# Attention and a gated MLP on one core: exponentials turned in 32x32 blocks on VectorE, v products in plain fp32 on eight array tiles

## The chip, the core and the metric

The kernel runs on one core of one Trainium2 chip. The core has five engines with a queue each: TensorE (PE in the profile; its weight loads are the row PEld), VectorE (DVE), ScalarE (ACT), GpSimd (POOL) and SyncE (SP), which here only issues DMAs. SBUF and PSUM have 128 partitions; TensorE reads SBUF and writes PSUM. The metric is the device time of one execution in microseconds (us).

## What is computed

Eight batches, eight heads, 576 positions, head size 64. Attention runs for each head, and its output feeds an MLP for each batch in which the positions are mixed by a 576x576 matrix.

```python
q_rot, k_rot = (rotate(q), rotate(k))
scores = scale * np.matmul(q_rot, k_rot.transpose(0, 1, 3, 2))
scores = scores - np.max(scores, axis=-1, keepdims=True)
attn = np.exp(scores)
attn = attn / (np.sum(attn, axis=-1, keepdims=True) + 1e-09)
x = np.matmul(attn, v)
...
h = np.maximum(x @ w_in, 0.0)
u, v = (h[..., :d_ff // 2], h[..., d_ff // 2:])
v_n = (v - mu) / np.sqrt(var + 1e-06)
v_s = np.einsum('ts,bsd->btd', w_spatial, v_n) + b_spatial[None, :, None]
out = (u * v_s) @ w_out
```

## The kernel before

**Tiling.** Two heads make a pair, so there are 32 pairs, four to a batch. A pair's scores are nine tiles of 128 query rows by 576 keys: four for each head, and a ninth that holds the last 64 queries of both. A score tile is a PSUM buffer of the pool `sc` (two of them). TensorE fills it (L542; for pair 0 L552), VectorE takes the negated row maximum `nmx` (L563), and ScalarE writes the exponentials `e` to SBUF and sums them (L565).

**Values.** The product with v contracts over keys, so keys must lie on partitions, while `e` has queries there. TensorE therefore turns `e` in 128x128 blocks by matmuls with an identity (`tp`, L582) into PSUM. To keep full precision in fp32r products, ScalarE rounds the turned block to `eh` (L593), and VectorE writes the rest to `el` (L312, a line shared by all such remainders). v is split in the same way into `vs` (ScalarE, then GpSimd L443). `pv` (L606) then sums `eh` by both parts of v, and `el` by the high part. The 576 queries of both heads are worked in three chunks of 384 columns. At the end of a chunk ScalarE copies one half of `pv` (L623) and VectorE adds the other (L621). The first four pairs (`PLAIN = 4`) skip the split: their products (L679) are plain fp32, 64 output rows wide, from turned blocks that ScalarE or VectorE copies out of PSUM (L648, L650). Then GpSimd multiplies by the inverse sums (L716), and `x` is split for the MLP.

**MLP.** For each batch there are four stages of fp32r products: `pa` (L750), `pb` (L773), `pc` (L791) and `pd` (L806), in PSUM banks of the pool `pm`. The turned blocks `tp` use the same pool.

**Order.** No queue is filled at run time by readiness. The program lists operations with a cost, a key (due time) and the buffers that they take. `Program.run` plays this list through once while the program is built: whenever an engine is free, it takes the ready operation with the lowest key whose buffers can be placed. The order so found is fixed for each engine, and each engine works through it in order. Pair i has keys from 20*i on, and the MLP of batch b from 80*b + 90.

```python
SLOTS = {
    "stage": 2, "lk": 1, "vraw": 2, "vs": 2, "e2": 4, "e1": 2, "eh": 7, "rb": 1, "x32": 1, "xg": 7, "m": 4,
    "small": 3, "nmx": 3, "rt": 2, "sc": 2, "pv": 1, "pm": 3,
}
```

The costs in that list are the author's figures for the planner. They are not measurements, and no time in this document is taken from them.

Of the kernel before, what the change touches and what calls it, by code (L numbers as in the profile page):

```python
# [9 lines left out]
F32 = mybir.dt.float32  # L10
# [6 lines left out]
P = 128  # L17
# [20 lines left out]
PSUM = {"sc": 1024, "pv": 512, "pm": 512}  # L38
# [6 lines left out]
CHUNKS = [  # L45
# [22 lines left out]
K_LOAD, K_ROPE, K_SUM, K_HIQ, K_LOQ, K_LOK, K_STACK, K_STACK2, K_V, K_VLO = 27, 8, 8, 9, 9, 11, 30, 8, -2, -9
# [31 lines left out]
class Op:  # L100
    def __init__(self, costs, key, f, new, port):
        self.costs, self.key, self.f, self.new, self.port = costs, key, f, new, port
        self.eng, self.late = None, 0
        self.waits, self.after, self.bufs = 0, [], []


class Program:
# [30 lines left out]
    def run(self, make):  # L138
# [22 lines left out]

        busy = dict.fromkeys(LATENCY, False)
# [5 lines left out]
        while events:  # L168
# [23 lines left out]
            for e in LATENCY:  # L192
# [3 lines left out]
                while ready[e] and not chosen:  # L196
# [27 lines left out]
def tile_attention_gated_mlp(  # L224
# [48 lines left out]
    ident = T([P, P], F32, "ident")  # L273
# [10 lines left out]
    ks = [T([P, TW + S], F32R, f"ks{a}") for a in range(2)]  # L284
# [95 lines left out]

    def prepare(i):
# [4 lines left out]
        st = [Buf("stage", [P, 2 * S + TW], F32, f"st{i}_{j}") for j in range(2)]  # L386
        lk = Buf("lk", [P, TW + S], F32R, f"lk{i}")
        vr = Buf("vraw", [P, NQ, 2, D], F32, f"vr{i}")
        vs = Buf("vs", [P, NQ, 2, 2, D], F32R, f"vs{i}")
        prepped.append((lk, vr if i < PLAIN else vs))  # L390

        def hi(j, rows=slice(0, P)):

            return st[j][rows, S:2 * S + TW * j].bitcast(F32R)
# [16 lines left out]
        op(DMA, 910, key - K_LOAD + 1, lambda: load(vr.tile, v[b, hp]), w=[vr], new=[vr])  # L411
# [28 lines left out]
        if i < PLAIN:  # L440
            return
# [507 lines left out]
```

## Time and profile before

The median of 3 runs is 967.17 us (965.44 to 967.69). The profiled execution's span is 963.6 us, 3.6 us below that median.

| engine | busy us | share of the span | main work |
|---|---|---|---|
| PE | 934.0 | 97% | MLP products, scores, turning `e`, v products |
| ACT | 738.2 | 77% | exponentials, rounding `eh` |
| DVE | 656.6 | 68% | row maxima, remainders `el` |
| POOL | 601.1 | 62% | rotation, remainders of q, k, x |

The table is to be read with care. A share is a mean over three parts: about 100 us with the first four pairs and no MLP, some 800 us with attention and MLP side by side, and a last part with the MLP of the last batch alone. PE's busy time also counts a matmul's pipeline, so overlapping matmuls each show more than their share; how far apart they start says more.

### The profile page before, as it was taken

How to read it: one execution, taken by the hardware profiler on the slowest of the kernel's cores; microseconds unless marked ns; L12 is line 12 of the kernel's file. 1: busy time of each engine (PE TensorE's matmuls, PEld its weight loads, DVE VectorE, ACT ScalarE, POOL GpSimd, SP SyncE). 2: the span in 40 equal slices, each digit the busy share in tenths (PEclk: the TensorE clock that was granted, in tenths of full speed). 3: DMA queues.
4: the chain of work that ended last, by engine and by line, in shares of the span. 5: the costliest groups of instructions: out<-in, count | busy, mean ns of one | idle time of the engine just before them, and what ended most of it. 6: DMA issues, size and time to landing. Idle time of an engine off the chain costs nothing.

```text
span 963.6 us, 19472 instructions
## 1 busy us (share of the span) xinstructions
PE 934.0 (97%) x6614; PEld 856.2 (89%) x6614; DVE 656.6 (68%) x1461; ACT 738.2 (77%) x1835; POOL 601.1 (62%) x526
## 2 busy tenths in 40 slices
PE   4988899999999999999999999999999999999998
PEld 2555589999899989999899998999889998999998
DVE  5898686766867677665776658676676766866331
ACT  4887788777987779777897779877798678976452
POOL 6775766576758557774765766666586765672121
PEclk9998999999999999999999999999999999999999
DMA  7775634455354554346444444445524455430101
GB/s 273 240 233 170 191 106 124 130 125 140 103 136 127 159 141 114 102 116 171 124 135 118 117 149 122 127 122 152 149 74 132 123 167 144 110 83 13 62 1 50
DMA packets 56037, 124.64 MB, mean 129 GB/s; under 512 B 13185, under 2 KB 13441, under 8 KB 55938
## 3 DMA queue, kind: packets, MB, share of 16 engines
q1 hardware_dynamic: 55938, 123.40, 46.0%
q8 instruction: 53, 0.87, 0.4%
q14 instruction: 46, 0.38, 0.1%
HBM read 66.03 MB, written 9.58 MB: 78 GB/s over the span
## 4 chain that ended last, share of the span: by engine, by line
PE 75%; ACT 13%; DVE 6%; issue 2%; DMA 2%; POOL 1%; SPq 0%; ACTq 0%; DVEq 0%; POOLq 0%
PE sc L542 13%; PE pc L791 12%; PE pv L606 11%; PE tp L582 11%; PE pd L806 10%; PE pb L773 9%; PE pa L750 5%; ACT e L565 4%; ACT eh L593 2%; DVE nmx L563 2%; ACT vv L837 2%; PE pv L679 1%; PE sc L552 1%; DVE el L312 1%; ACT st L309 1%
## 5 line engine op out<-in xcount | busy, mean ns | idle before, releaser
L593 ACT ACTIVATE eh<-tp 128x384 fp32r<-128x384 f32 (+1 forms) x504 | 217.9, 434 | 85.4 <-PE tp L582 68.2
L312 DVE TENSOR_TENSOR el<-tp,eh 128x384 fp32r<-128x384 f32 x336 | 185.9, 554 | 101.9 <-ACT eh L593 88.0
L563 DVE TENSOR_REDUCE nmx<-sc 128x1 f32<-128x576 f32 x288 | 214.9, 749 | 47.9 <-PE sc L542 40.7
L565 ACT ACTIVATE e<-sc,nmx 128x576 f32<-128x576 f32 x288 | 213.2, 741 | 40.1 <-DVE nmx L563 36.0
L582 PE MATMUL tp<-ident,e 128*128 128x128 f32 (+1 forms) x1176 | 195.6, 273 | 1.3 <-DVE eh L312 0.4
L401 POOL TENSOR_TENSOR st<-st,tabq 128x576 f32<-128x576 f32 x62 | 87.9, 1435 | 134.0 <-DMA st<-in_qk_dram 104.5
L582 PEld LDWEIGHTS tp<-ident,e 128*128 128x128 f32 (+1 forms) x1176 | 145.8, 138 | 16.3 <-issue 3.0
L606 PE MATMUL pv<-eh,vs 128*128 128x384 f32 (+1 forms) x560 | 154.5, 317 | 1.5 <-ACT x L685 1.4
L791 PE MATMUL pc<-wsp,vn 128*128 128x288 f32 x768 | 143.1, 303 | 0.0
L773 PE MATMUL pb<-x,wi 128*128 128x288 f32 x768 | 141.8, 306 | 0.6 <-ACT u L776 0.5
L806 PE MATMUL pd<-g,wo 128*128 128x288 f32 x768 | 141.3, 303 | 0.0
L542 PE MATMUL sc<-ks,qs 128*128 128x288 f32 x620 | 133.1, 304 | 4.8 <-ACT e L565 4.3
L750 PE MATMUL pa<-wi,x 128*128 128x512 f32 x448 | 133.2, 407 | 0.0
L542 PE MATMUL sc<-lk,qz 128*128 128x288 f32 x558 | 120.4, 297 | 0.0
L806 PEld LDWEIGHTS pd<-g,wo 128*128 128x128 f32 x768 | 114.0, 189 | 3.4 <-DVE el L312 0.4
L791 PEld LDWEIGHTS pc<-wsp,vn 128*128 128x128 f32 x768 | 114.6, 189 | 1.8
L773 PEld LDWEIGHTS pb<-x,wi 128*128 128x128 f32 x768 | 112.1, 189 | 4.4 <-PE pb L773 1.1
L542 PEld LDWEIGHTS sc<-ks,qs 128*128 128x128 f32 x620 | 100.8, 190 | 15.9 <-ACT e L565 7.2
L606 PE MATMUL pv<-el,vs 128*64 128x384 f32 (+1 forms) x448 | 113.9, 295 | 0.1
L606 PEld LDWEIGHTS pv<-eh,vs 128*128 128x128 f32 x560 | 97.7, 188 | 7.8 <-DVE x L621 2.0
L716 POOL TENSOR_TENSOR x<-x,rb 128x576 f32<-128x576 f32 x32 | 45.9, 1435 | 79.2 <-DVE x L621 73.1
L312 DVE TENSOR_TENSOR eh<-tp,eh 64x256 fp32r<-64x256 f32 (+1 forms) x168 | 59.8, 356 | 51.8 <-ACT eh L593 28.2
(166 smaller groups left out, 1540.6 us busy)
## 6 DMA issues: line engine op xcount, KB each, us to landing
st<-in_qk_dram SPq DMA_DIRECT2D x64, 576.0 KB
ks<-st SPq DMA_DIRECT2D x124, 160.0 KB
qs<-st SPq DMA_DIRECT2D x124, 144.0 KB
vr<-in_v_dram SPq DMA_DIRECT2D x32, 320.0 KB
qz<-st SPq DMA_DIRECT2D x62, 144.0 KB
out_dram<-ob SPq DMA_DIRECT2D x31, 288.0 KB
ws<-in_w_spT_dram SPq DMA_DIRECT2D x2, 576.0 KB
tabs<-in_tab_dram SPq DMA_DIRECT2D x1, 576.0 KB
```

Source lines behind the costliest of these rows:

```text
L312: eng.tensor_tensor(out=lo, in0=src, in1=hi.bitcast(F32), op=ALU.subtract)
L401: f = lambda e: e.tensor_tensor(out=st[j][:, cols], in0=st[j][:, cols], in1=(tabs if j else tabq)[:, cols], op=ALU.mult)
L542: nc.tensor.matmul(pt[:, c * 512:c * 512 + HALF], lhsT=lhsT, rhs=rhs[:, k0 + c * HALF:k0 + (c + 1) * HALF], start=(n == 0), stop=(n == len ...
L563: op(DVE, 665, key + K_MAX, lambda: nc.vector.tensor_reduce(out=nmx.tile, in_=tops(), op=ALU.max, axis=AX.XY, negate=True), r=[pt], w=[nmx ...
L565: op(ACT, 730, key + K_EXP, lambda: nc.scalar.activation(e[:, e0:e0 + S].rearrange("p (c n) -> p c n", c=2), tops(), AF.Exp, bias=nmx.tile ...
L582: nc.tensor.transpose(out=tp[:e.shape[1], m * P:m * P + P], in_=e, identity=ident)
L593: nc.scalar.activation(h, p, AF.Copy)
L606: nc.tensor.matmul(pv[0:rows, c1:c2], lhsT=vs[:, kt, h, vp, :], rhs=part[:, c1:c2], start=(kt == 0 and n == 0 and c1 == 0), stop=last)
L750: nc.tensor.matmul(pm.tile, lhsT=lhsT, rhs=win[1, d][:, j, :], start=(d == 0 and n == 0), stop=(d == 3 and n == len(todo) - 1))
L773: nc.tensor.matmul(pm[:, :HALF], lhsT=win[0, d][:, i, f * P:(f + 1) * P], rhs=x[d][:, at:at + HALF], start=(d == 0 and n == 0), stop=(d == ...
L791: nc.tensor.matmul(pm[:, :HALF], lhsT=lhsT, rhs=rhs, start=(t == 0 and n == 0), stop=(t == 4 and n == 1))
L806: nc.tensor.matmul(pm[:, :HALF], lhsT=wout[d,][:, i, m * P:(m + 1) * P], rhs=gs[d][:, at:at + HALF], start=(d == 0 and n == 0), stop=(d == ...
```

## The change

Three things replace the way to the v products, for all pairs alike.

**Turning on VectorE.** ScalarE writes all nine exponential tiles of a pair into one buffer `et` (two of them exist). VectorE turns each tile in place, as 4x18 blocks of 32x32. After that, the 32 partitions of a group g hold 32 keys of a block b for the 32 queries of group g; the identity, its matmuls, `eh`, `el`, `vs` and all their copies go.

**Plain fp32 products in eight tiles of the array.** For each of the 18 key blocks, eight matmuls run with 32 rows (group g) and 64 output columns (head h), 160 or 128 columns moving. They sum into four banks, one for each g, and into the upper or lower half by h. These are 144 matmuls a pair, issued as one operation that takes all four `pm` banks. The banks are a single tile now, the pool `pv` is gone, and `pm` has four slots.

**v four times.** Each group of 32 partitions needs every key block, so v is loaded into each of the four groups by a DMA of its own.

The rest follows from this. A ScalarE copy of three instructions brings the four banks to `x32`. The planner lets the 144 matmuls reserve their banks: while they wait for one, no other operation may take a `pm` slot. k is stored without its extra 64 columns, and the MLP waits for the batch's last pair at its start.

```diff
-    "stage": 2, "lk": 1, "vraw": 2, "vs": 2, "e2": 4, "e1": 2, "eh": 7, "rb": 1, "x32": 1, "xg": 7, "m": 4,
-    "small": 3, "nmx": 3, "rt": 2, "sc": 2, "pv": 1, "pm": 3,
+    "stage": 2, "lk": 1, "vrep": 1, "et": 2, "rb": 1, "x32": 1, "xg": 7, "m": 4,
+    "small": 3, "nmx": 3, "rt": 2, "sc": 2, "pm": 4,
...
+                    elif waiting and item[2] is not waiting[0] and any(b.pools[0] == waiting[0].new[0].pools[0] for b in item[2].new):
+                        passed.append(item)
...
+                        if item[2].reserve and not waiting:
+                            waiting.append(item[2])
...
+            rows = v[b, hp].rearrange("(q j) k h d -> j q (k h d)", q=4)
+            for g in range(4):
+                load(vr[32 * g:32 * g + 32].rearrange("j q k h d -> j q (k h d)"), rows)
...
-        op(ACT, 627, key + K_V, lambda: round_hi(vs[:, :, :, 0, :], vr.tile), r=[vr], w=[(vs, 0)], new=[vs])
...
+        et = Buf("et", [P, 9, S], F32, f"et{i}")
+        for n, (a, t) in enumerate(TILES):
+            scores(i, a, t, qk_low, sm, et, key + S_STEP * n, [et] if n == 0 else [])
+        pv = [Buf("pm", None, None, f"pv{i}_{g}") for g in range(4)]
+
+        def multiply():
+            parts = [(0, 0, 0, 5, 32), (1, 0, 0, 5, 32), (2, 1, 4, 9, 0), (3, 1, 4, 9, 0), (2, 0, 0, 4, 32), (3, 0, 0, 4, 32), (0, 1, 5, 9, 32), (1, 1, 5, 9, 32)]
+            for b in range(NB):
+                for g, h, s0, s1, c0 in parts:
+                    rows = slice(32 * g, 32 * g + 32)
+                    at = 512 * g + c0
+                    nc.tensor.matmul(banks[64 * h:64 * h + 64, at:at + 32 * (s1 - s0)], lhsT=vr[rows, b % 4, b // 4, h, :], rhs=et[rows, s0:s1, 32 * b:32 * b + 32], start=(b == 0), stop=(b == NB - 1))
+
+        o = op(PE, 5200, key + K_AV, multiply, r=[vr, *[(et, n) for n in range(9)]], w=pv, new=pv)
+        o.reserve = True
+
+        def copy():
+            by_bank = banks.rearrange("p (g n) -> p g n", g=4)
+            whole = by_bank[:, :, 32:160].rearrange("p g (t i) -> p g t i", i=32)
+            nc.scalar.activation(x32[:, :4 * P].rearrange("p (t g i) -> p g t i", t=4, g=4), whole, AF.Copy)
+            for h, g, c0 in ((0, 0, 160), (1, 2, 0)):
...
+        op(DVE, 670, key + K_TURN, lambda: nc.vector.transpose(out=et[:, at, :], in_=et[:, at, :]), w=[(et, at)])
...
-                ahead = [(x[2], 0), (x[2], 1)] if d == 0 else []
+                ahead = [(x[3], 0), (x[3], 1)] if d == 0 else []
```

**What stands where.** The first place is TensorE's queue around the values of pair 11 before. `tp` are turned blocks, `eh` and `el` the split exponentials, `sc` scores, `pd` and `g` the last MLP stage. The piece is one of many like it.

```order
L606 MATMUL pv_0_4368<-el_0_2_4350,vs_3928 64x384
L542 MATMUL sc_1_2_4414<-ks_79,qs_77 128x288 x2
L542 MATMUL sc_1_2_4414<-lk_4008,qz 128x288 x2
L806 MATMUL pd_01_4423<-g_0_3948,wo_1051 128x288 x3
L582 MATMUL tp_1_1_4429<-ident,e_11_1_4262 128x128 x2
L582 MATMUL tp_1_1_4429<-ident,e_11_1_4354 128x128
L806 MATMUL pd_01_4423<-g_1_4081,wo_807 128x288 x3
L606 MATMUL pv_0_4368<-eh_0_3_4376,vs_3928 128x384
```

Here turning, v products, scores and MLP alternate in small pieces. The same queue in the changed program, from the last scores of pair 12 to its values (`banks` at L487; the two rows of that line shown recur 18 times):

```order
L658 MATMUL banks<-g_3_4260,wo_2047 128x288 x3
L516 MATMUL sc_1_2_4646<-ks_79,qs_77 128x288 x2
...
L516 MATMUL sc_0_3_4656<-ks_78,qs_76 128x288 x2
...
L516 MATMUL sc_1_3_4668<-ks_79,qs_77 128x288 x2
...
L516 MATMUL sc_0_4_4683<-ks_78,qs_76 128x288 x2
...
L516 MATMUL sc_0_4_4683<-lk_4349,qz 128x288 x2
L487 MATMUL banks<-et_4406,vr_4591 64x160 x4
L487 MATMUL banks<-et_4406,vr_4591 64x128 x4
```

The values moved into one block of 144 matmuls. At this place it stands right behind the pair's last scores, with four score tiles and no MLP product ahead of it; at most other places MLP products stand between.

The second place is the start of TensorE's queue in the changed program, with the scores of pairs 0 and 1 and the first block of values:

```order
L525 MATMUL sc_0_4_208<-st_1_90,st_0_97 64x288 x4
L516 MATMUL sc_0_0_230<-ks_78,qs_76 128x288 x2
...
L516 MATMUL sc_0_4_335<-lk_204,qz 128x288 x2
L487 MATMUL banks<-et_114,vr_99 64x160 x4
L487 MATMUL banks<-et_114,vr_99 64x128 x4
...
L516 MATMUL sc_0_0_531<-ks_78,qs_76 128x288 x2
```

Before, pair 0's turning and products stood among the scores of pair 1. Now all nine score tiles of pair 1 come ahead of pair 0's values, and the scores of pair 2 behind them.

The third place is VectorE. Before, around the end of pair 16:

```order
L312 TENSOR_TENSOR el_1_0_6584<-tp_1_0_6569,eh_1_0_6577 128x384
L563 TENSOR_REDUCE nmx_1_3_6593<-sc_1_3_6579 128x1
L828 BN_STATS sm_0_6608<-vv_0_6600 128x6
L312 TENSOR_TENSOR el_1_1_6619<-tp_1_1_6595,eh_1_1_6605 128x384
```

In the changed program, in the middle of a pair's scores:

```order
L536 TENSOR_REDUCE nmx_0_2_8641<-sc_0_2_8485 128x1
L539 STREAM_TRANSPOSE et_8457<-et_8457 128x576 x2
L536 TENSOR_REDUCE nmx_1_0_8673<-sc_1_0_8654 128x1
L536 TENSOR_REDUCE nmx_1_1_8679<-sc_1_1_8668 128x1
L539 STREAM_TRANSPOSE et_8457<-et_8457 128x576 x2
```

The remainders `el` went; nine turns of a whole tile in SBUF came, each behind an exponential of ScalarE instead of a matmul of TensorE.

More of the change, by code (lines that the diff above doesn't have):

```diff
@@ L487, in prepare_whole @@
-        op(DMA, 910, key - K_LOAD + 1, lambda: load(vr.tile, v[b, hp]), w=[vr], new=[vr])
+        load_values(vr, b, hp, key)
     def attention(i):
-        b, hp = pairs[i]
-        lk, vs = prepped[i]
+        key = 20 * i
+        qk_low, vr = prepped[i]
         sm = sums[i % 2]
         x32 = Buf("x32", [P, S], F32, f"x32_{i}")
-        todo = []
-        for c, (tiles, spans) in enumerate(CHUNKS):
-            key = 20 * i + 20 / 3 * c
-            e2 = Buf("e2", [P, 2 * S], F32, f"e2_{i}_{c}")
-            e1 = Buf("e1", [P, S], F32, f"e1_{i}_{c}")
-            for n, (a, t) in enumerate(tiles):
-                scores(i, a, t, lk, sm, key + S_AT[n], e1 if n == 2 else e2, n)
-            todo.append((key + K_T, c, spans, e2, e1))
@@ L529, in scores @@
+        op(ACT, 900, key + K_AV + K_COPY, copy, r=pv, w=[x32], new=[x32])
+        normalise(i, sm, x32, key)
+    def scores(i, a, t, lk, sm, et, key, new):
         pt = Buf("sc", None, None, f"sc{i}_{a}_{t}")
         nmx = Buf("nmx", [P, 1], F32, f"nmx{i}_{a}_{t}")
-        k0 = TW * (n_e != 1)
-        e0 = S * (n_e == 1)
         def mm():
@@ L550, in mm_whole @@
                     rows = slice(0, P) if t < 4 else own
-                    kc = k0 + c * HALF
-                    nc.tensor.matmul(pt[rows, c * 512:c * 512 + HALF], lhsT=q[own, q0:q0 + rows.stop - rows.start], rhs=kf[own, kc:kc + HALF], start=True, stop=True)
+                    nc.tensor.matmul(pt[rows, c * 512:c * 512 + HALF], lhsT=q[own, q0:q0 + rows.stop - rows.start], rhs=kw[own, c * HALF:(c + 1) * HALF], start=True, stop=True)
         def tops():
@@ L564, in scores @@
+        op(PE, 8 * pe_ns(HALF) if i < WHOLE else 4 * pe_ns(HALF) if t < 4 else 6 * pe_ns(HALF), key, mm_whole if i < WHOLE else mm, r=[*need, *([] if new else [(et, "first")])], w=[pt, *([(et, "first")] if new else [])], new=[pt, *new])
+        op(DVE, 750, key + K_MAX, lambda: nc.vector.tensor_reduce(out=nmx.tile, in_=tops(), op=ALU.max, axis=AX.XY, negate=True), r=[pt], w=[nmx], new=[nmx])
         at = 5 * a + t
-        op(ACT, 730, key + K_EXP, lambda: nc.scalar.activation(e[:, e0:e0 + S].rearrange("p (c n) -> p c n", c=2), tops(), AF.Exp, bias=nmx.tile, scale=1.0, accum_out=sm[:, at:at + 1]), r=[pt, nmx, *([(e, 0)] if n_e == 1 else [])], w=[(e, n_e), ("sums", i % 2, at)], new=[] if n_e == 1 else [e])
@@ L689, in normalise @@
+        op(ACT, 740, key + K_EXP, lambda: nc.scalar.activation(et[:, at, :].rearrange("p (c n) -> p c n", c=2), tops(), AF.Exp, bias=nmx.tile, scale=1.0, accum_out=sm[:, at:at + 1]), r=[pt, nmx], w=[(et, at), ("sums", i % 2, at)])
+        op(DVE, 670, key + K_TURN, lambda: nc.vector.transpose(out=et[:, at, :], in_=et[:, at, :]), w=[(et, at)])
     def normalise(i, sm, x32, key):
@@ L714, in normalise @@
         op(DMA, 2000, key + K_GET, get, r=[(rt, 1)], w=[rb], new=[rb])
-        whole = [(x32, c) for c in range(len(CHUNKS))]
+        whole = [x32]
         pair_op(S, key + K_X, lambda e: e.tensor_tensor(out=x32.tile, in0=x32.tile, in1=rb.tile, op=ALU.mult), r=[rb], w=whole)
@@ L857, in tile_attention_gated_mlp @@
     pairs = [(b, hp) for b in range(B) for hp in range(NP)]
-    prepped, xs, chain = [], [], []
-    op(POOL, 800, -80, lambda: make_identity(nc, ident), w=["ident"])
+    prepped, xs = [], []
     op(POOL, 800, -26, setup, w=["bias", ("sums", 0, 0), ("sums", 1, 0), ("qz", 0), ("qz", 1), ("qs", 0, 0), ("qs", 1, 0)])
-    for n in range(0):
-        idle = Buf("pv", None, None, f"idle{n}")
-        wide = lambda: ident.rearrange("p (o n) -> p o n", o=1).to_broadcast([P, 4, P])
-        op(PE, 1600, 10000 + n, lambda idle=idle: nc.tensor.matmul(idle.tile.rearrange("p (c n) -> p c n", c=4), lhsT=ident, rhs=wide(), start=True, stop=True), r=["ident"], w=[idle], new=[idle])
     prepare(0)
```

219 lines of the change are left out of this document (37 added, 182 removed), and 3 rows, old and new, of the table CHUNKS.

## The prediction

> **What bounds the kernel now.** I read the page first, then the waits of the middle part, then stretches of time, and last the timeline of TensorE, for how far apart matmuls start.
>
> ```profile
> PE 934.0 (97%) x6614; PEld 856.2 (89%) x6614; DVE 656.6 (68%) x1461; ACT 738.2 (77%) x1835; POOL 601.1 (62%) x526
> PE tp L582 <- DVE eh L312: 0.4, 1, 0.4
> PE pb L773 <- ACT u L776: 0.2, 1, 0.2
> 0.00:60.00 60.00, 44.33 (x236) 27.64 (x237) 46.06 (x75) 41.37 (x95) 40.10 (x47) 1.00 0.79 253
> 400.00:500.00 100.00, 99.69 (x719) 93.74 (x717) 70.31 (x165) 80.97 (x205) 65.88 (x57) 1.00 0.50 134
> ```
>
> The two waits are all that TensorE has between 120 and 900 us, 0.6 us together. In the stretch from 400 to 500 us it is busy for 99.69 of 100 us (first engine column), with no other engine over 81. So there a microsecond of TensorE is a microsecond of the kernel, and relief of ScalarE or VectorE is worth nothing. Only the first 60 us leave TensorE idle (44.33 of 60).
>
> **What goes from TensorE.**
>
> ```profile
> 401.35 0.34 PE L606 MATMUL pv<-eh,vs 128*128 128x384 f32 x1
> 401.53 0.34 PE L606 MATMUL pv<-el,vs 128*64 128x384 f32 x1
> 401.70 0.55 PE L791 MATMUL pc<-wsp,vn 128*128 128x288 f32 x3
> 407.75 0.96 PE L791 MATMUL pc<-wsp,vn 128*128 128x288 f32 x6
> 408.55 0.49 PE L582 MATMUL tp<-ident,e 128*128 128x128 f32 x3
> 417.90 0.49 PE L582 MATMUL tp<-ident,e 128*128 128x128 f32 x3
> 418.14 1.04 PE L791 MATMUL pc<-wsp,vn 128*128 128x288 f32 x6
> 419.03 0.43 PE L791 MATMUL pc<-wt,vt 128*128 128x288 f32 x2
> ```
>
> First column: start; second: length with its pipeline. Starts tell the price: `pv` takes 0.18 and 0.17 us, six `pc` take 0.80 (0.133 each), and three `tp` with six `pc` take 1.13, so a `tp` takes 0.11. A pair has 42 `tp` (4.6 us) and 27 `pv` of 384 columns (4.7 us). That is 9.4 us a pair, for 28 pairs.
>
> **What comes to TensorE: 144 plain fp32 products.** The trace of before has such products in other tile sizes.
>
> ```profile
> 95.33 0.54 PE L679 MATMUL pv<-et_0a,vr 128*64 128x384 f32 x1
> 95.33 0.54 PE L679 MATMUL pv<-et_0b,vr 128*64 128x384 f32 x1
> 95.70 0.49 PE L679 MATMUL pv<-et_0a,vr 128*64 128x384 f32 x1
> 95.71 0.49 PE L679 MATMUL pv<-et_0b,vr 128*64 128x384 f32 x1
> 96.02 0.49 PE L679 MATMUL pv<-et_1a,vr 128*64 128x384 f32 x1
> 74.86 0.86 PE L679 MATMUL pv<-et,vr 64*64 64x384 f32 x4
> 75.65 0.53 PE L542 MATMUL sc<-ks,qs 128*128 128x288 f32 x2
> ```
>
> A product shows twice: plain fp32 is two passes, each with its own weight load. A pass of 384 columns takes 0.32 us (95.70 to 96.02), 0.83 ns a column. Halves of the array side by side run at once (two starts at 95.33), and so do quarters: the four passes of two 64x64 products take 0.79 us, not four times 0.32. If all eight tiles run at once, the longest one needs 18 x 2 x 160 x 0.83 ns = **4.8 us** a pair. That is the lower end.
>
> But the block has 288 passes and 288 loads, 576 instructions. In 4.8 us they would have to reach the array every 8.3 ns. How fast does TensorE's sequencer hand them over?
>
> ```profile
> 67.62 0.31 PEld L641 LDWEIGHTS tp_1a<-ident,e 128*128 128x128 f32 x3 [0.81 <-ACT et_0b L648]
> 67.62 0.55 PE L641 MATMUL tp_1a<-ident,e 128*128 128x128 f32 x3 [0.58 <-ACT et_0b L648]
> 679.73 0.31 PEld L582 LDWEIGHTS tp<-ident,e 128*128 128x128 f32 x3 [0.59 <-PE pd L806]
> 679.76 0.52 PE L582 MATMUL tp<-ident,e 128*128 128x128 f32 x3 [0.39 <-DVE eh L312]
> ```
>
> The first load and its matmul at 67.62 had waited in the queue, and start together. At 679.73 the sequencer itself had waited, so nothing was queued: the same matmul starts 0.03 us behind its load. I read this as 30 ns an instruction when none are in store. 576 x 30 ns = 17.3 us, the upper end for a dispatch-bound block. Some are in store while the block waits for the last turn, so I take **15 us**, near the row's 17.3. So instead of 9.4 us, 28 pairs pay 15: 28 x 5.6 = **+157 us**.
>
> The Trainium skill, "TensorE: Matmul & The Clock Gate", section "Wait — 56ns, not 53.3ns?", gives 62 ns of sequencer work per MATMUL with hardware decode off, and a floor of 25 ns either way; by the first, 288 passes would take an estimated 17.9 us, by the second 7.2. The trace's 30 ns from load to matmul, two to a pass, agree with the first.
>
> **VectorE and ScalarE.**
>
> ```profile
> L563 DVE TENSOR_REDUCE nmx<-sc 128x1 f32<-128x576 f32 x288 | 214.9, 749 | 47.9 <-PE sc L542 40.7 <-PE sc L552 4.2 <-PE tp L641 0.6
> L457 DVE TENSOR_TENSOR kf<-st 128x576 f32<-128x576 f32 x1 | 0.8, 757 | 0.0
> L711 DVE RECIPROCAL sums<-sums 128x9 f32<-128x9 f32 x32 | 6.5, 204 | 1.8 <-ACT sums L710 1.8
> L712 DVE STREAM_TRANSPOSE rt<-sums 128x32 f32<-128x32 f32 x32 | 6.5, 204 | 0.4
> L312 DVE TENSOR_TENSOR el<-tp,eh 128x384 fp32r<-128x384 f32 x336 | 185.9, 554 | 101.9 <-ACT eh L593 88.0 <-PE pv L606 3.8 <-PE pb L773 3.2
> L824 ACT ACTIVATE vv<-pa 128x512 f32<-128x512 f32 x32 | 19.2, 599 | 10.9 <-PE pa L750 10.7
> ```
>
> A turn of 128x32 takes 204 ns, as much as a reciprocal of nine columns, so most of it is fixed. A turn of 576 columns lies between 0.2 and 18 x 0.204 = 3.7 us; I take the 0.75 us of L457, an SBUF operation of that size. 288 turns are 216 us for the 186 of `el` and more that go: VectorE stays under TensorE, with 1.5 us a score tile. The copy of the four banks costs ScalarE 0.6 us (L824) and two small ones, about 1 us. 504 `eh` copies go, off the path. v's loads grow from 320 to 1280 KB a pair; they have a pair's time, some 28 us, to land, and cost nothing unless SP, in order, holds back the q and k loads behind them.
>
> **New waits on TensorE.** The block takes all four `pm` banks, so the MLP's last bank must be emptied before, and the copy must end after. Before the block that is some 0.5 us and a semaphore. Behind it two score tiles (2 x 0.53 us) cover the copy of 1 us. I take 0.8 us a pair, 28 x 0.8 = 22 us; with full cover it is nothing, without any 2 us. Behind the block stand the next pair's scores and the MLP, and on ScalarE the next exponentials stand behind the copy, so both engines stop with it. At some places, the second piece of rows in the section on the change, the block also waits for scores without MLP to cover them: eight score tiles at 1.5 us on VectorE and a tail of some 3 us (maximum, exponential, turn) against 7.7 us of TensorE's work (scores 4.5, 24 MLP products 3.2). That is 8 us, three times, and once 10: 34 us. Together **+56 us**.
>
> **The start.**
>
> ```profile
> 102.08 0.97 PE L750 MATMUL pa<-wi,x 128*128 128x512 f32 x3
> 30.00:105.00 75.00, 65.73 (x416) 42.45 (x415) 68.74 (x118) 60.14 (x145) 51.31 (x46) 0.95 0.72 215
> L353 DVE SCALAR_TENSOR_TENSOR dcwi<-dcwi,sgwi 128x512 f32<-128x512 f32 x8 | 5.5, 692 | 0.0
> ```
>
> The first MLP product starts at 102 us, and VectorE is the fullest until then (68.74 of 75 us). After, it has 36 x 1.5 = 54 us of maxima and turns, and weight decoding of six instructions at 0.69 us, some 6.5 slices: 27 us. That is about what it has now. But decoding needs a `pm` bank, and `et` has two buffers, so VectorE stops for most of each block: four times 12 us. **+50 us**.
>
> **The sum.** 963.6 (span) + 157 + 56 + 50 = 1226.6. The median stands 3.6 us over the span: **1230 us**.
>
> **The rivals.**
>
> *The array is the bound after all*, faster. If the sequencer keeps up with 8.3 ns, a block is 5 us: 28 x (5 - 9.4) = -123, start +16 (turns, and four waits of 2 us), waits +56: 963.6 - 123 + 16 + 56 + 3.6 = 916 us. For it: loads and passes in other tiles start within 10 ns of each other when queued (95.33, 95.70 and 95.71). Against: the 30 ns. It decides below 6.8 us a block. 22%. The Trainium skill, "TensorE: Matmul & The Clock Gate", section "The mechanism", has tiles start 4 ns apart, which is this case; no row here shows it over 576 instructions.
>
> *Loads ride free*, only passes pay 30 ns: 8.6 us a block; 28 x (8.6 - 9.4) = -22, start +30, waits +56: 1031 us. For it: only the gap from load to matmul is shown. 15%. The floor of 25 ns in the Trainium skill, cited above, would put this rival at an estimated 7.2 us a block and 990 us.
>
> *The clock falls.* A thin array could lose its clock.
>
> ```profile
> L552 PE MATMUL sc<-kf,st 64*128 64x288 f32 x32 | 12.5, 724 | 12.8 <-DVE st L474 9.6 <-ACT e L565 3.2
> 79.95 0.69 PE L542 MATMUL sc<-lk,qz 128*128 128x288 f32 x2
> 86.86 0.43 PE L542 MATMUL sc<-lk,qz 128*128 128x288 f32 x2
> ```
>
> After a pause, scores took 0.69 us instead of 0.43 from 79 to 86 us. If each block leaves 7 us at half speed, 3.5 us x 28 = 98 more: 1328 us. 10%.
>
> *The tiles run one after another*, the change's word not kept: 18 x 2 x 1152 x 0.83 ns = 34.4 us a block, some 1850 us. The rows of 74.86 and 95.33 speak against it. 3%.
>
> **Chances.** 50% for my forecast, 1230 (1160 to 1290, as a block is 13 to 17 us); 22, 15, 10 and 3 for the others. A measurement here tells 0.2% from no change. Faster 0.21, within 0.2% 0.02, slower 0.77. The range reaches down into the first rival, whose own range is 890 to 940, and stops below the clock case: **900 to 1300** leaves out some 4 below, 10 and 3 above.
>
> **What would show it.** The L487 group: passes of one block starting 52 ns apart on average, with ScalarE and VectorE idle behind it, confirm the step; passes 17 ns apart give the array. Turns of 0.75 us, TensorE waiting for turns about 8 us at the named places, and a granted clock of 1.00 confirm the rest. A turn over 2 us would make VectorE the bound and the forecast wrong.

## The result, and the profile after

The changed kernel takes **1172.8 us** (1163.8 to 1180.0, four runs) against 966.3 us: 1.213 times as long, 95% interval 1.206 to 1.220. The medians here are of fast runs; of the kernel with v loaded once, one slower run (1004.3 us) is left out. The forecast was 1230 us, slower. The sign and the range held, and the sum was 5% off. But its largest term was some 207 us too high and its waits some 142 us too low, so that the sum came out close by luck.

The profiled execution has a span of 1162.0 us, 198.4 more than before. First the page's rows of busy time and of instruction transfers (packets, MB, share):

```profile
PE 900.9 (78%) x13314; PEld 780.3 (67%) x13314; DVE 572.1 (49%) x1086; ACT 502.0 (43%) x1230; POOL 545.5 (47%) x461
q8 instruction: 105, 1.72, 0.6%
```

TensorE has twice the instructions and is busy for 33 us *less* than before (934.0). Its idle time rose from 29.6 to 261.1 us: the loss is waiting, not work. The stretches of time, with the same columns as those shown of before:

```profile
0.00:60.00 60.00, 32.28 (x348) 23.57 (x348) 37.78 (x58) 25.79 (x54) 34.09 (x37) 1.00 0.79 233
60.00:120.00 60.00, 33.23 (x670) 28.45 (x670) 40.26 (x64) 25.46 (x61) 29.68 (x24) 0.70 0.74 196
120.00:200.00 80.00, 53.62 (x738) 42.31 (x738) 45.06 (x88) 34.30 (x79) 33.57 (x27) 0.78 0.41 99
700.00:800.00 100.00, 83.56 (x1264) 73.75 (x1263) 51.39 (x107) 47.57 (x119) 55.81 (x47) 0.97 0.56 142
```

In the middle TensorE works 84 of 100 us where it worked 99.69, and no other engine is over 56: nothing is full. In the start the granted clock (third column from the end) is 0.70 and 0.78; before it was 0.94 from 60 to 120 us and 1.00 after:

```profile
60.00:120.00 60.00, 51.64 (x324) 34.37 (x322) 48.69 (x83) 45.82 (x114) 44.01 (x38) 0.94 0.64 190
120.00:200.00 80.00, 79.79 (x580) 75.35 (x579) 58.73 (x140) 64.78 (x161) 52.90 (x46) 1.00 0.42 114
```

What TensorE waits for in the changed kernel, longest first, without one single wait of 11.4 us at the start (total us, times, longest):

```profile
PE banks L487 <- issue: 51.1, 40, 3.5
PE sc L516 <- ACT et L538: 32.4, 44, 2.4
PE banks L643 <- DVE u L705: 24.9, 46, 0.7
PE banks L625 <- ACT u L628: 17.7, 34, 0.6
PE banks L658 <- ACT ob L661: 16.7, 33, 0.6
PE banks L602 <- ACT vv L676: 14.3, 24, 1.4
PE banks L487 <- DVE et L539: 11.2, 3, 4.1
```

Two kinds of wait here were not in the forecast. One is "issue", inside the blocks of values. The other is four rows of one form: an MLP stage (L602, L625, L643, L658) waits for ScalarE or VectorE to empty a bank, 74 us in 137 short waits. (The last row is the blocks' wait for turns, which the forecast had.) TensorE's weight loads over some 11 us in the middle (start, length, what; in brackets the idle time before) show both:

```profile
646.95 1.23 PEld L643 LDWEIGHTS banks<-wsp,vn 128*128 128x128 f32 x9 [0.78 <-DVE u L705]
648.13 0.32 PEld L643 LDWEIGHTS banks<-wt,vt 128*128 128x128 f32 x2
648.39 0.46 PEld L643 LDWEIGHTS banks<-wsp,vn 128*128 128x128 f32 x3
649.70 0.43 PEld L643 LDWEIGHTS banks<-wsp,vn 128*128 128x128 f32 x3 [0.85 <-DVE u L705]
650.08 0.32 PEld L643 LDWEIGHTS banks<-wt,vt 128*128 128x128 f32 x2
651.20 4.04 PEld L487 LDWEIGHTS banks<-et,vr 32*64 32x64 f32 x234 [0.81 <-issue]
657.55 0.88 PEld L487 LDWEIGHTS banks<-et,vr 32*64 32x64 f32 x54 [2.31 <-issue]
```

Here each group of MLP products begins with a pause of its weight loads of 0.8 us. The block then runs 234 loads and as many passes in 4.04 us, **8.6 ns an instruction**, stands for 2.31 us, and runs the last 54 loads. Over all 32 pairs a block takes 7.6 us, 5.7 to 10.1 by the trace. The operations that the forecast priced from other rows (busy, mean ns, idle before):

```profile
L539 DVE STREAM_TRANSPOSE et<-et 128x576 f32<-128x576 f32 x288 | 218.5, 770 | 73.7 <-ACT et L538 73.4
L495 ACT ACTIVATE x<-banks 128x512 f32<-128x512 f32 x32 | 19.1, 598 | 181.6 <-PE banks L487 181.6
```

A turn takes 0.77 us (0.75 forecast), the large copy 0.60 (0.6). The first MLP product, from the timeline:

```profile
139.72 1.65 PE L602 MATMUL banks<-wi,x 128*128 128x512 f32 x3 [2.12 <-DVE sgwi L345]
```

It starts 38 us later than before (102.08).

To see where time goes in a kernel with four pairs to a batch, I use VectorE's 32 reciprocals (one a pair). Times from the traces, in us, the later kernels being those of the experiments:

| kernel | to the 8th | 8th to 32nd | 32nd to the end | span |
|---|---|---|---|---|
| before | 208.9 | 684.2 | 70.5 | 963.6 |
| changed | 288.7 | 772.9 | 100.4 | 1162.0 |
| four tiles | 253.1 | 700.4 | 71.9 | 1025.4 |
| four tiles, v loaded once | 246.7 | 674.3 | 70.6 | 991.6 |
| four tiles, pieces | 245.2 | 682.2 | 73.4 | 1000.8 |
| four tiles, pieces and numbers | 226.9 | 666.4 | 81.0 | 974.3 |

The change costs 80 us up to the eighth pair, 89 in the steady part and 30 at the end.

### The profile page after: what moved, and what is told of

The parts are those of the page before. It is cut to its first block, busy times and chain, and to the rows that moved or that the text cites. A ratio compares the mean times of both kernels' runs of the same rounds, so it can differ in the third digit from the quotient of the medians.

```text
span 1162.0 us, 31490 instructions
## 1 busy us (share of the span) xinstructions
PE 900.9 (78%) x13314; PEld 780.3 (67%) x13314; DVE 572.1 (49%) x1086; ACT 502.0 (43%) x1230; POOL 545.5 (47%) x461
## 4 chain that ended last, share of the span: by engine, by line
PE 52%; ACT 9%; DVE 7%; issue 6%; DMA 6%; SPq 3%; POOL 2%; DVEq 0%; ACTq 0%; POOLq 0%
PE banks L487 13%; PE banks L625 10%; PE banks L643 9%; PE banks L658 7%; PE sc L516 7%; PE banks L602 6%; SPq L301 3%; ACT et L538 2%; DVE u L705 2%; DVE nmx L536 2%; DMA vr<-in_v_dram 2%; ACT u L628 1%; DVE et L539 1%; ACT vv L676 1%; ACT ob L661 1%
## 5 line engine op out<-in xcount | busy, mean ns | idle before, releaser
L538 ACT ACTIVATE et<-sc,nmx 128x576 f32<-128x576 f32 x288 | 211.7, 737 | 144.6 <-DVE nmx L536 143.3
L539 DVE STREAM_TRANSPOSE et<-et 128x576 f32<-128x576 f32 x288 | 218.5, 770 | 73.7 <-ACT et L538 73.4
L487 PE MATMUL banks<-et,vr 32*64 32x160 f32 (+1 forms) x9216 | 194.3, 311 | 72.4 <-issue 51.1
L487 PEld LDWEIGHTS banks<-et,vr 32*64 32x64 f32 x9216 | 174.5, 140 | 91.2 <-issue 63.5
L516 PE MATMUL sc<-ks,qs 128*128 128x288 f32 x620 | 148.0, 331 | 56.2 <-ACT et L538 32.4
L625 PE MATMUL banks<-x,wi 128*128 128x288 f32 x768 | 137.4, 321 | 39.9 <-ACT u L628 17.7
L516 PEld LDWEIGHTS sc<-ks,qs 128*128 128x128 f32 x620 | 105.9, 205 | 80.9 <-ACT et L538 50.0
L625 PEld LDWEIGHTS banks<-x,wi 128*128 128x128 f32 x768 | 117.2, 204 | 59.5 <-ACT u L628 28.4
L643 PE MATMUL banks<-wsp,vn 128*128 128x288 f32 x768 | 127.1, 302 | 25.5 <-DVE u L705 23.5
L658 PE MATMUL banks<-g,wo 128*128 128x288 f32 x768 | 124.2, 303 | 22.9 <-ACT ob L661 16.7
L602 PE MATMUL banks<-wi,x 128*128 128x512 f32 x448 | 123.1, 410 | 21.3 <-ACT vv L676 14.3
L643 PEld LDWEIGHTS banks<-wsp,vn 128*128 128x128 f32 x768 | 107.3, 188 | 37.0 <-DVE u L705 32.8
L658 PEld LDWEIGHTS banks<-g,wo 128*128 128x128 f32 x768 | 105.9, 188 | 36.2 <-ACT ob L661 26.3
L516 PE MATMUL sc<-lk,qz 128*128 128x288 f32 x558 | 128.9, 315 | 0.0
L602 PEld LDWEIGHTS banks<-wi,x 128*128 128x128 f32 x448 | 80.6, 192 | 46.4 <-ACT vv L676 22.3
L516 PEld LDWEIGHTS sc<-lk,qz 128*128 128x128 f32 x558 | 98.6, 207 | 0.8 <-issue 0.8
```

The source lines that it names most:

```text
L487: nc.tensor.matmul(banks[64 * h:64 * h + 64, at:at + 32 * (s1 - s0)], lhsT=vr[rows, b % 4, b // 4, h, :], rhs=et[rows, s0:s1, 32 * b:32 * ...
L516: nc.tensor.matmul(pt[:, c * 512:c * 512 + HALF], lhsT=lhsT, rhs=rhs[:, c * HALF:(c + 1) * HALF], start=(n == 0), stop=(n == len(parts) - 1))
L538: op(ACT, 740, key + K_EXP, lambda: nc.scalar.activation(et[:, at, :].rearrange("p (c n) -> p c n", c=2), tops(), AF.Exp, bias=nmx.tile, s ...
L539: op(DVE, 670, key + K_TURN, lambda: nc.vector.transpose(out=et[:, at, :], in_=et[:, at, :]), w=[(et, at)])
L602: nc.tensor.matmul(pm.tile, lhsT=lhsT, rhs=win[1, d][:, j, :], start=(d == 0 and n == 0), stop=(d == 3 and n == len(todo) - 1))
L625: nc.tensor.matmul(pm[:, :HALF], lhsT=win[0, d][:, i, f * P:(f + 1) * P], rhs=x[d][:, at:at + HALF], start=(d == 0 and n == 0), stop=(d == ...
```

## The experiments

**One tile or four.** In the diff, the four `pm` banks became slices of one tile, `banks`, so that one ScalarE instruction can copy from all four. Is that what makes each MLP group wait for the one before, though it uses another bank?

```diff
-    banks = ps.tile([P, 4 * 512], F32, tag="banks", name="banks", bufs=1)
...
-        if b.pool == "pm":
-            return banks[:, 512 * b.slot:512 * b.slot + 512]
...
-                    nc.tensor.matmul(banks[64 * h:64 * h + 64, at:at + 32 * (s1 - s0)], lhsT=vr[rows, b % 4, b // 4, h, :], rhs=et[rows, s0:s1, 32 * b:32 * b + 32], start=(b == 0), stop=(b == NB - 1))
+                    nc.tensor.matmul(pv[g].tile[64 * h:64 * h + 64, c0:c0 + 32 * (s1 - s0)], lhsT=vr[rows, b % 4, b // 4, h, :], rhs=et[rows, s0:s1, 32 * b:32 * b + 32], start=(b == 0), stop=(b == NB - 1))
...
-            nc.scalar.activation(x32[:, :4 * P].rearrange("p (t g i) -> p t g i", t=4, g=4), whole, AF.Copy)
+            for g in range(4):
+                nc.scalar.activation(x32[:, :4 * P].rearrange("p (t g i) -> p g t i", t=4, g=4)[:, g], pv[g].tile[:, 32:160].rearrange("p (t i) -> p t i", i=32), AF.Copy)
```

> Same arithmetic; the four pm banks are four PSUM tiles instead of four slices of one tile, and the copy of the output is eight ScalarE instructions (one or two a bank) instead of three. Theory A (the one tile makes every MLP group's first matmul wait until the group before it has been emptied, although it uses another bank): the waits of TensorE for ScalarE and VectorE ahead of L602, L625, L643 and L658, 14.3 + 17.7 + 24.9 + 16.7 = 74 us in the changed kernel, fall below 15 us, decoding no longer holds up the start, and the time falls from 1173 to between 1050 and 1110 us. Rival B (the emptying engines are late in any case, so the wait comes back when the same bank is used again): the waits stay above 50 us together and the time stays within 2% of 1173. Rival C (stalls of 0.25 to 3.8 us inside the blocks, each at the 193rd of 256 instructions, 51 us by the page, are the whole loss): the time stays above 1150 whatever the waits do. In every case the gaps inside the blocks stay near 51 us.

The control keeps the one tile and makes only the copy into the same eight instructions.

> Control for the run with four tiles: the changed kernel with its single tile, and only the copy of the output in eight ScalarE instructions instead of three. All theories: ScalarE has 5 more instructions of 0.2 to 0.3 us a pair, so 0 to 1.5 us a pair on 32 pairs, and the time is between 1173 and 1225 us. If it is faster than 1173 by over 1%, the gain of the run with four tiles isn't all due to the tiles.

With four tiles: **1029.7 us**, 1.066 of before (1.063 to 1.069). The control: 1174.7 us, 1.214 (1.211 to 1.217), so the copy's form costs nothing that can be measured. TensorE's rows for the four MLP stages with four tiles:

```profile
L620 PE MATMUL pb<-x,wi 128*128 128x288 f32 x768 | 116.8, 303 | 3.9 <-DVE vv L605 2.6
L653 PE MATMUL pd<-g,wo 128*128 128x288 f32 x768 | 115.5, 301 | 4.0 <-POOL g L303 2.9
L597 PE MATMUL pa<-wi,x 128*128 128x512 f32 x448 | 116.9, 401 | 1.8 <-POOL x L303 1.2
L638 PE MATMUL pc<-wsp,vn 128*128 128x288 f32 x768 | 116.3, 297 | 0.8 <-issue 0.8
```

The same four groups in the changed kernel:

```profile
L625 PE MATMUL banks<-x,wi 128*128 128x288 f32 x768 | 137.4, 321 | 39.9 <-ACT u L628 17.7
L643 PE MATMUL banks<-wsp,vn 128*128 128x288 f32 x768 | 127.1, 302 | 25.5 <-DVE u L705 23.5
L658 PE MATMUL banks<-g,wo 128*128 128x288 f32 x768 | 124.2, 303 | 22.9 <-ACT ob L661 16.7
L602 PE MATMUL banks<-wi,x 128*128 128x512 f32 x448 | 123.1, 410 | 21.3 <-ACT vv L676 14.3
```

The idle time ahead of them (after the second bar) is 10.5 us together with four tiles, and 109.6 with one. Theory A holds in its main part, and the gain is more than I expected: 137 us of span, 36 in the start, 72 in the steady part and 28 at the end. The order of work is the same in both but for the copy's instructions, and each bank still waits for its own emptying; what went are waits between operations on different banks. Only the early start did not come: the first MLP product still begins at 137 us.

```profile
137.16 0.87 PE L597 MATMUL pa<-wi,x 128*128 128x512 f32 x3
```

That is 3 us earlier than with one tile and 35 later than before, so the 36 us of the start were gained behind it. Rival C fell as the whole loss, but its gap stayed as expected: 49.1 us.

**The gap inside the blocks.** In the changed kernel 38 stalls in blocks have 58.8 us by the trace, and every one begins at TensorE's 193rd instruction of 256, counted from the first of the program, those that only wait or branch included. To see the rate of a long block, each was issued four times over:

```diff
-            for b in range(NB):
+            for b in [*range(NB)] * 4:
```

> The block of each pair is issued four times over (the sums start anew each time, so the outputs are the same): 2304 instructions of 64 bytes, 147 KB, instead of 576. Theory C (TensorE runs out of instructions, because 256 instructions, 16 KB, are used up in 2.2 us at 8.5 ns each and fetched more slowly): stalls at every 256th instruction, nine in a block, each of some 1 to 4 us; the instruction queue's packets rise from 105 to about 320, and a block takes 2304 x 8.5 ns = 19.6 us plus nine stalls, 30 to 45 us; the time grows by 32 x (22 to 37) us, to 1880 to 2360 us. Rival (the stalls come from what the kernel does beside the block, a queue of transfers that is full just then): the stalls a block stay at about 1.2, a block takes 20 to 24 us, and the time is 1650 to 1750 us. Rival D (30 ns an instruction once nothing is in store, the prediction's step): spacing grows from 8.5 ns to 30 ns after the first few hundred instructions, 60 us a block.

One run took 1954.9 us. One block in the timeline, weight loads only:

```profile
1719.95 4.04 PEld L487 LDWEIGHTS banks<-et,vr 32*64 32x64 f32 x239 [0.16 <-ACT u L628]
1725.49 2.15 PEld L487 LDWEIGHTS banks<-et,vr 32*64 32x64 f32 x128 [1.49 <-issue]
1728.96 2.15 PEld L487 LDWEIGHTS banks<-et,vr 32*64 32x64 f32 x128 [1.32 <-issue]
1732.43 2.15 PEld L487 LDWEIGHTS banks<-et,vr 32*64 32x64 f32 x128 [1.32 <-issue]
1735.90 2.15 PEld L487 LDWEIGHTS banks<-et,vr 32*64 32x64 f32 x128 [1.32 <-issue]
1739.64 2.15 PEld L487 LDWEIGHTS banks<-et,vr 32*64 32x64 f32 x128 [1.60 <-issue]
```

And the page's row of instruction transfers:

```profile
q8 instruction: 321, 5.26, 1.2%
```

After the first pause the block runs in equal portions: 128 loads and 128 passes in 2.15 us, a pause of 1.3 to 1.6 us, and again, 3.47 to 3.75 us a portion. The second row says what a portion is: 321 packets of 5.26 MB are 16.4 KB each, 256 instructions of 64 bytes (81924 TensorE instructions times 64 bytes are 5.24 MB). So TensorE uses instructions up at 8.4 ns each and gets them at 13.6 to 14.6 ns. Of 257 stalls, 256 begin at the 193rd of 256; together they last 394.7 us. The packets' own times agree: in the changed kernel's 38 stalls, which last from 0.25 to 3.8 us, TensorE goes on 1.20 to 1.54 us after the end of a packet of this queue, whatever the stall's length. That is theory C, near the low end of its time. The rival of a busy queue and the 30 ns an instruction (rival D, the prediction's step) fall.

**Room for the fetch.** On top of four tiles, the block was issued in three pieces with due times of their own, so that the planner can put score tiles between.

```diff
-        o = op(PE, 5200, key + K_AV, multiply, r=[vr, *[(et, n) for n in range(9)]], w=pv, new=pv)
-        o.reserve = True
+        for n in range(3):
+            o = op(PE, 1800, key + K_AV + 5 * n, lambda n=n: multiply(range(6 * n, 6 * n + 6)), r=[vr, *[(et, n) for n in range(9)]], w=pv, new=[] if n else pv)
+            o.reserve = not n
```

> The kernel with four tiles (1029.7 us), its block issued in three pieces of 192 instructions, between which the planner may put score tiles of the next pair (0.55 us of TensorE each, 8 to 10 instructions). Theory C (stalls inside the blocks are instruction fetch; a refill of 256 instructions takes about 3.6 us in the run with blocks four times as long, against the 2.2 us in which a block uses them up): two score tiles between the pieces give the fetch 1.1 us, so the idle time of the L482 group put down to issue falls from 49 us to between 15 and 30 us, and the time by 20 to 35 us, to 995 to 1010 us. Rival (scores put there are only taken from behind the block, where they covered the copy of the output, or wait themselves for their score buffers): the issue time falls but waits for ScalarE at the scores' line grow by as much, and the time stays within 1% of 1029.7.

1009.3 us, 1.045 of before (1.040 to 1.051). The block's row in the groups of the kernel with four tiles:

```profile
L482 PE MATMUL pv<-et,vr 32*64 32x160 f32 (+1 forms) x9216 | 199.7, 311 | 64.9 <-issue 49.1
```

And with three pieces:

```profile
L482 PE MATMUL pv<-et,vr 32*64 32x128 f32 (+1 forms) x9216 | 212.3, 311 | 52.0 <-issue 29.6
```

The issue time falls by 19.5 us and the time by 20.4, as theory C expected, at the low end; the rival's return in score waits did not come (38.6 to 27.9 us), though waits for q copies rose (11.8 to 20.7). The planner ordered everything anew here, so that the two figures agree is less than a proof.

**The planner's numbers.** The planner of the changed kernel reckons 5.2 us for a block, and this was set to what the trace shows, with three other costs; first alone, then with the pieces.

```diff
-        o = op(PE, 5200, key + K_AV, multiply, r=[vr, *[(et, n) for n in range(9)]], w=pv, new=pv)
+        o = op(PE, 7500, key + K_AV, multiply, r=[vr, *[(et, n) for n in range(9)]], w=pv, new=pv)
...
-        op(ACT, 900, key + K_AV + K_COPY, copy, r=pv, w=[x32], new=[x32])
+        op(ACT, 2000, key + K_AV + K_COPY, copy, r=pv, w=[x32], new=[x32])
```

> The kernel with four tiles; only the planner's numbers for four steps are set to what the trace shows (block 7500 ns instead of 5200, copy 2000 for 900, turn 780 for 670, v load 5500 for 3000), so the order of instructions changes and nothing else. Theory F (the order was planned for blocks a third too short, so that score tiles wait for ScalarE, 38.6 us, and SP's queue stands 122 us for blocks that the planner thought done): these two fall by a third or more and the time falls by 10 to 30 us. Rival (what waits is set by the dependences and the one v buffer, whatever the order): the time stays within 1% of 1029.7, or grows as an order for slower engines leaves gaps.

> Three pieces and the planner's numbers together (2300 ns a piece). If both gains are real and independent, the time is the sum of the two runs' gains: 965 to 1000 us, which may reach the 966 us of the kernel before. If they cover the same waits, it is that of the better one, within 0.5%.

Alone: 1025.8 us, 1.064 (1.059 to 1.069), no change. Theory F falls: waits at scores rose from 38.6 to 41.9 us, and SP's for blocks only fell from 122 to 113. With the pieces: **978.7 us**, 1.014 (1.011 to 1.017), the fastest of this study, and still slower than before. The gain of 51 us is twice the sum of the two alone (24), so they are not independent. In the steady part this kernel is 18 us faster than the one before (666.4 against 684.2); it loses 18 in the start and 10 at the end. Why numbers that did nothing alone gave 31 us with the pieces, I did not settle. By the table 18 us of it lie before the eighth pair, where the first MLP product begins at 141 us instead of 167, and 16 in the steady part; the end is 8 longer.

**v's loads.** In the kernel with four tiles, three of the four loads of v went for all pairs but the first.

```diff
+    kept = T([P, 4, NQ, 2, D], F32, "kept")
...
+        if b.pool == "vrep":
+            return kept
...
-            for g in range(4):
+            for g in range(4 if key == 0 else 1):
```

> The kernel with four tiles, but three of the four copies of v are loaded for the first pair alone, into one tile that is kept; so each later pair multiplies three quarters of its exponentials with v of the first pair, and the outputs are others. 31 pairs load 320 KB of v instead of 1280. Theory D (the larger v load costs time: bytes at the start, where the DMA share is 0.79 and 0.75 in the first two minutes of 60 us, and the queue held behind it): the time falls by 15 to 45 us, most of it before 185 us, and the half clock of 60 to 120 us (0.72) rises. Rival E (v's load lies beside other work; the start is late because decoding, exponentials and turns share VectorE and ScalarE): the time falls by less than 8 us, and 60 to 120 us look as they did.

993.4 us, 1.028 (1.024 to 1.033) against 1.066: v's loads cost 36 us by the runs' times and **34 us** by the spans of the two traces, so rival E falls. But by the table only 6 of the 34 lie before the eighth pair and 26 in the steady part, where I had not expected them; the clock from 60 to 120 us stayed low (0.70 after 0.72). TensorE's waits for q and k with four tiles, and with v loaded once:

```profile
PE sc L511 <- DMA qs<-st: 11.8, 5, 10.8
PE sc L511 <- DMA ks<-st: 8.0, 4, 2.4
PE sc L515 <- DMA qs<-st: 9.8, 7, 6.1
PE sc L515 <- DMA ks<-st: 3.1, 3, 1.3
```

They fall by 7 us, so waiting for q and k is a small part of the 34, whatever delays the copies. More runs asked whether the order of SP's queue (D1) or the bytes (D2) cost it, all from the kernel of 978.7 us. First, ScalarE issues the loads:

```diff
-                load(vr[32 * g:32 * g + 32].rearrange("j q k h d -> j q (k h d)"), rows)
+                (nc.scalar if key else nc.sync).dma_start(out=vr[32 * g:32 * g + 32].rearrange("j q k h d -> j q (k h d)"), in_=rows)
...
+            op(ACT, 250, key - 20 + K_AV + K_COPY, fetch, r=[("vl", key - 20)], w=[vr, ("vl", key)], new=[vr]).late = 5500
```

> The kernel with three pieces and the planner's numbers (978.7 us, 1.014 of the kernel before); the four v loads of each pair but the first are issued by ScalarE right behind the copy of the pair before, instead of by SP, which stands 154 us between 200 and 900 us for blocks (the one v buffer must come free). Theory D1 (the 34 us that v's loads cost in the run with v loaded once come from what SP, in order, holds back behind them: the q and k loads): TensorE's waits for the q and k copies (qs and ks, 35 us in the whole run) fall by half or more, and the time falls by 8 to 25 us, under 966. Theory D2 (they come from the bytes, 960 KB a pair more on the same transfer engines): the time stays within 0.8% of 978.7, and the waits for q and k stay. Issuing costs ScalarE itself under 0.5 us a pair.

1114.3 us, 1.152 (1.148 to 1.155). ScalarE and its queue at one pair's copy:

```profile
408.89 0.45 ACTq L377 DMA_DIRECT2D vr<-in_v_dram  x1
409.03 0.57 ACT L497 ACTIVATE x<-pv 64x32 f32<-64x32 f32 x4
416.68 1.04 ACTq L377 DMA_DIRECT2D vr<-in_v_dram  x2
417.77 0.74 ACT L537 ACTIVATE et<-sc,nmx 128x576 f32<-128x576 f32 x1 [8.17 <-DMA ks<-st]
```

Between its second and third load ScalarE stands 7 us, and the next exponential with it; over the run exponentials wait 175 us in this way for q and k copies that SP issued. The trace shows what the load waits for: the semaphore with which it will report its own end, and which a transfer of SP was using until then. The program gives the same eight semaphores to the transfers of both engines, and 27 of ScalarE's loads stand 3 to 8 us for one, 169 us together. So the run tests this sharing and says nothing between D1 and D2. In the second, SP keeps v's loads, but they are due 22 units later.

```diff
-        op(DMA, 5500, key - K_LOAD + 1, fetch, w=[vr], new=[vr])
+        op(DMA, 5500, key + (K_AV - 20 if key else 1 - K_LOAD), fetch, w=[vr], new=[vr])
```

> The same kernel with SP still issuing v's loads, but due 22 planner units later (a pair is 20), so that the planner puts the q and k loads ahead of v's where both are ready. D1: as much gain as from ScalarE's queue where SP's order was the cause, 5 to 25 us; and SP's wait for blocks falls below 100 us between 200 and 900 us. D2: within 0.8% of 978.7; if v then lands too late, TensorE waits for v (4.2 us before) and the time grows.

994.3 us, 1.028 (1.025 to 1.031) against 1.014: slower. TensorE's waits for q and k stay (20.8 and 14.2 us against 21.2 and 13.4), its wait for v grows from 4.2 to 7.1, and SP's for blocks falls only to 130 us. That speaks against D1, as far as a new order of everything allows.

In the third, ScalarE makes three of the four copies of v from the one that is loaded, for all pairs or for the first five alone:

```diff
+            nc.scalar.activation(to, own, AF.Copy)
...
-        op(DMA, 5500, key - K_LOAD + 1, fetch, w=[vr], new=[vr])
+        op(DMA, 2500 if key >= 0 else 5500, key - K_LOAD + 1, fetch, w=[(vr, c) for c in range(7)], new=[vr])
+        if key >= 0:
+            for c in range(6):
+                op(ACT, 1120, key + 8 + c, lambda c=c: repeat(c), r=[(vr, 6)], w=[(vr, c)])
```

> The kernel with three pieces and the planner's numbers (978.7 us, 1.014 of the kernel before), and for every pair only one copy of v is loaded; ScalarE makes the other three from it, six copies of 32x1280 of an estimated 1.1 us (by 0.6 us for 512 columns), 6.7 us a pair, on an engine that is busy 52% of its time. Theory D2 (the extra 960 KB a pair are what costs in v's load: 34 us in the run with v loaded once): transfers fall from 155 to about 125 MB, TensorE's waits for q and k copies (qs and ks, some 35 us) fall by half, and the time falls by 10 to 30 us, to 949 to 969: level with the kernel before or faster. Rival (ScalarE's copies of 1.1 us stand ahead of exponentials, and TensorE waits for scores' buffers instead): ScalarE's share rises to some 75%, TensorE's waits for ScalarE ahead of scores grow by more than 20 us, and the time stays or grows.

> The same, but ScalarE makes the copies for the first five pairs alone, where transfers are busiest (DMA share 0.82 and 0.83 in the first two stretches of 60 us) and ScalarE least; the later pairs load v four times as before. D2: the fifth reciprocal, at 127 us in the run with pieces and numbers, and the sixth at 167 us come 5 to 12 us earlier, and the time is 965 to 975 us. Rival (the start is bound by decoding, and by TensorE at half clock): less than 3 us earlier, and 976 to 982 us.

All pairs: 1061.1 us, 1.097 (1.093 to 1.102). First five: 1021.4 us, 1.059 (1.053 to 1.065). The page's row of transfers with copies for all pairs:

```profile
DMA packets 56081, 123.40 MB, mean 116 GB/s; under 512 B 13185, under 2 KB 13441, under 8 KB 55938
```

Two of TensorE's waits there:

```profile
PE sc L520 <- ACT et L542: 58.9, 37, 8.6
PE pv L490 <- DVE wi L303: 21.1, 6, 5.8
```

And ScalarE's copies among the groups:

```profile
L382 ACT ACTIVATE vr<-vr 32x1280 f32<-32x1280 f32 x192 | 237.8, 1266 | 8.0 <-DMA vr<-in_v_dram 5.2
```

TensorE's waits for q and k, 34.6 us, are gone, as D2 said; but a kernel 82 us slower also gives these copies more time, so that the bytes did it is not shown. And the rival took more: in nine pairs all six copies stand in a row and hold the exponentials up for 7.3 us, the wait at scores goes from 19.3 to 58.9 us, and the start is later still in both runs (fifth reciprocal at 171 us against 127; with copies for all pairs the DMA share is 0.29 from 60 to 120 us). So with few transfers the start is not faster while ScalarE stands in the way; whether it would be, without that, stays open.

**Six pieces**, from the kernel with three pieces and numbers.

```diff
-        for n in range(3):
-            o = op(PE, 2300, key + K_AV + 5 * n, lambda n=n: multiply(range(6 * n, 6 * n + 6)), r=[vr, *[(et, n) for n in range(9)]], w=pv, new=[] if n else pv)
+        for n in range(6):
+            o = op(PE, 1200, key + K_AV + 5 * n, lambda n=n: multiply(range(3 * n, 3 * n + 3)), r=[vr, *[(et, n) for n in range(9)]], w=pv, new=[] if n else pv)
```

The due times of the pieces stay 5 units apart, so that the last is now due 25 units after the first, where a pair has 20.

> The kernel with three pieces and the planner's numbers, but six pieces of 96 instructions, so up to five score tiles may lie inside a block. Theory C: idle time put down to issue in the block's group falls from 24 us to under 12 us, and the time by 5 to 12 us, to 967 to 974 us. Rival (score buffers are what limits: two, and a score tile takes VectorE 1.5 us, so no more than one or two fit into a block): the issue time and the time stay within 0.5%, or the time grows because the four banks are held longer.

1024.5 us, 1.060 (1.055 to 1.064). The issue time fell to 17.5 us, not under 12, and these grew, from 21.2 and 4.2 us with three pieces:

```profile
PE sc L512 <- DMA qs<-st: 34.4, 14, 11.4
PE pv L482 <- DMA vr<-in_v_dram: 12.9, 13, 2.4
```

The rival's sign is right, but it was not score buffers: banks are held longer (a block takes 10.9 us from first to last product, on average, where it took 9.4), and loads come late. The run changes the number of pieces, their due times and the order of everything, so it does not show how many pieces are best.

## Why the prediction was right, and where it was wrong

**The block was mis-sized: the step that failed.** "I read this as 30 ns an instruction when none are in store" took the gap between one load and its matmul for the rate of a long row of instructions. In the block they follow at some 8.5 ns, close to the 8.3 ns that the lower end needed. A block took 7.6 us, of which 576 times 8.5 ns are 4.9, the stalls 58.8 / 32 = 1.8, and about half of the rest is the price of stretches at half clock (16.7 ns an instruction by the trace). So the term is 28 x (7.6 - 9.4) = **-50 us**, not +157. The rival "the array is the bound" had the rate in the block right (its 5 us for the 4.9 without stalls), but not the block of 7.6 us and not the 916 us; the one by which only the passes pay 30 ns fell too.

The figures of the Trainium skill, "TensorE: Matmul & The Clock Gate", section "Wait — 56ns, not 53.3ns?", 62 ns a matmul with hardware decode off and at least 25 either way, do not hold here: over eight tiles a pass starts every 17 ns. Its section "The mechanism", starts of other tiles 4 ns apart, is nearer to the trace, which shows 8.5 ns where load and pass alternate and the array itself needs 8.3.

**The waits were the loss.** Beside the block the span grew by 198.4 + 50 = 248 us, where I had 56 + 50 = 106. The missing 142 are nearly the 137 us of the one tile. I saw in the diff that the block needs all four banks, and priced the emptying before and behind it at 22 us; I did not ask what else is ordered by a tile that holds all banks, which is every MLP group. With four tiles the same plan takes 1030. That the sum came within 5% is luck: 207 us too much for the block and 142 too little for the waits.

**Scores ahead of blocks** were found at the right places and priced too high: 34 us forecast, 24 in the trace. Ahead of the blocks at 442.6, 706.3 and 961.5 us TensorE waits 1.5 to 1.6 us for exponentials, and each block 3.5 to 4.1 for its last turn (the row L487 <- DVE et of the waits), 5.1 to 5.6 us together where I had 8. The fourth place, nine score tiles ahead of the block at 234.8 us, has 8.4 us of waits where I had 10. Of the 32.4 us that TensorE waits for exponentials at L516, only 13 lie at these places. (The forecast's own terms, 8 x 1.5 + 3 - 7.7, give 7.3 us and not 8. And with 34.4 us a block its sum gives some 1770 us for the last rival; the step to 1850 isn't worked out.)

**The start** was too small: 80 us to the eighth pair for 50. With four tiles 36 of the 80 went, but the first MLP product came no more than 3 us earlier. In TensorE's queue that product stands behind the fourth block of values, which begins at 126.1 us with one tile and at 125.0 with four; what makes the first four blocks so late stays open. The half clock is there, at 0.70 and 0.78, not behind each block as the clock rival had it: in the middle the clock is 0.97.

**v's loads** "cost nothing unless SP holds back the q and k loads": they cost 34 us in the kernel with four tiles. That the condition is the cause is not shown, and TensorE's waits for q and k have only 7 of them.

**Turns and copy** came as priced.

**Instruction fetch** had no place in the forecast. It is 51 us by the page, 58.8 by the stalls in the trace.

## What to carry to other kernels

A tile is a unit of waiting: making one tile of several buffers to save an instruction orders all their users, and here that was two thirds of the loss, for a copy whose eight-instruction form cost nothing that could be measured. Price a row of many small instructions at three rates, that of the array, of the hand-over and of the fetch, and look for a rate in a long row, not in a gap between two. When several orders of a planned kernel differ by some per cent with no one wait to show for it, as here with the planner's numbers, a single variant says little about the cause that it was meant to test.

## What the runs showed of the hardware

- Loads and passes to eight array tiles of 32x64 follow each other at 8.4 to 8.6 ns at full clock, for over 400 instructions in a row, and at 16.7 ns in stretches at half clock.
- TensorE's instructions come in packets of 16.4 KB, 256 instructions, over transfers of their own queue; in a long block a portion takes 3.47 to 3.75 us, 1.3 to 1.6 of them standing still. In the run with blocks four times as long this made 13.6 to 14.6 ns an instruction, where the array took one every 8.4 as long as it had them. A stall ends 1.20 to 1.54 us after the end of such a packet in the changed kernel.
